# A planned transformer block on one core: 15 attention tiles moved from VectorE to ScalarE, weight copies moved off GpSimd, and a new instruction order

## The chip, the cores and the metric

The kernel runs on one core of a Trainium2 chip. The metric is the device time of one execution in microseconds (us), as a median of several executions. PE is TensorE (matrix products), ACT is ScalarE (exponentials, GELU, copies), DVE is VectorE, POOL is GpSimd, SP is the engine that issues the transfers.

## The reference, cut to what matters

One sequence of 2048 rows by 640 columns in bf16 goes through attention with 32 heads of 20 columns, then a gated feed-forward part of width 1728.

```python
x = A_x                                       # [1, 2048, 640]
qkv = layernorm(x) @ wqkv                     # 3 x 32 heads x 20
p = softmax(q @ k.T * 20 ** -0.5)             # per head, 2048 x 2048
h = x + (p @ v).reshape(1, 2048, 640) @ wo
g, u = layernorm(h) @ w_gate, layernorm(h) @ w_up      # 2048 x 1728
out = h + (gelu(g) * u) @ w_down
```

The scores are 32 x 2048 x 2048 numbers, and each goes through an exponential.

## The kernel before, in words

**Who sets the order.** The kernel is written as a list of operations with reads, writes, a duration and a priority (`op`). While the program is built, a planner (`Sched.schedule`) plays these through with its own durations, gives each engine a fixed order, hands out the 8 PSUM banks, and emits one stream for each engine with semaphore waits between them. On the chip each engine then runs its stream strictly in that order. So a planner number such as `c_dve` (VectorE), `c_act` (ScalarE) or the 0.222 us that it reckons for a group of score products adds no instruction; it only moves instructions within their streams. Priorities run from `P_QK` = 0 (first) over `P_PV` = 1 and `P_EPI` = 2 to `P_BG` = 3 (background).

**Tiling.** The query rows are cut into 7 chunks of 512, 512, 256, 256, 256, 128 and 128 rows (`CHUNKS`). The heads lie in 8 groups of 4, `g` = 0 to 7. A slot is one chunk of queries with as many head groups as fill 512 columns; there are 32 slots: 0 to 7 for chunk 0, 8 to 15 for chunk 1, then four each for the 256-row chunks and two each for the 128-row chunks. Each slot has 64 tiles of 128 keys x 512 columns, 2048 tiles in all. Consecutive tiles are joined to units of 2 or 3 tiles: a unit's score products (a "QK group" on PE) fill 2 or 3 banks, and one ACT instruction takes the exponential of the whole unit into bf16 (`pts`, or the second part of the ring in `rege`). Units alternate between banks 0 to 2 and banks 3 to 5. The string `PATS` says for each slot whether units alternate 3, 2 tiles ('2') or 3, 3 tiles ('3'). Where units are 3, 2, bank 5 is left to background work beside bank 7.

**VectorE tiles.** To relieve ACT, some tiles get their exponential on DVE from a polynomial on int16 bits (`d_exp`: one reading of PSUM for each tile, then seven instructions for a pair of tiles). The string `DS` gives their number for each slot (a hexadecimal digit), 217 of 2048 tiles in all; a unit of 3 with such a tile leaves a 2-tile exponential for ACT.

**Background.** While ACT takes exponentials, PE and DVE do everything else: `proj` makes the keys and queries of the next head group, `proj_v` the values, and `post` the output product, LayerNorm and feed-forward part of the chunk before. GELU of a chunk is done by ACT in one go, with a load of its function table before and after. Where PE has nothing to do, the planner fills in idle matmuls (`ps<-wo,gk`).

**Prologue.** Before the first QK group, all 16 blocks of 128 rows are normalised (statistics on the engines of `LNS`, scaling `LNE`), transposed on PE and copied out of PSUM (`LNV`: the copies `regw<-ps`) into `xnT`. Then `proj` makes the keys of head group 0 in four pieces (`k`, 0, 0 to 3) and the queries (`q`, 0, 0), on the engines of `G0E`; each key piece is squared (`sq`), summed by PE against `gk`, and its maximum (`kmx`, then `kq`, `fold`, `khalf`) is added to the queries, which the first QK group needs. The q and k weights come in packed at 20 columns a head and must lie at 32 columns a head (`wq_pad`, `wk_pad`). The function `pad` copies them: head group 0 early, the other 28 heads (`h0` = 4 to 32) in 5 pieces each for k and q, all on POOL, after the last scalings (`pad_ops`). These ten are called the weight copies below; `proj` of head group 1 needs all five of its kind.

```python
pad_ops.extend(x for x in e_ops[-8::2])
for dst, off, key in pads:
    for a in range(NA):
        pad(dst, off, 4, 32, key + "m", key, a, a + 1)
```

**Tail.** After the last exponential, the last chunk's 128 rows go through the output product, LayerNorm and feed-forward with nothing else to hide behind; ACT loads the tables for square root and GELU there.

Of the kernel before, what the change touches and what calls it, by code (L numbers as in the profile page):

```python
# [5 lines left out]
ACT = mybir.ActivationFunctionType  # L6
# [12 lines left out]
DMA_RATE = 0.36  # L19
DT = 0  # L20
LATE = (0, 1, 2, 3, 4)
LNS = [{'a': 'act', 'd': 'dve'}[x] for x in 'dddadddadddaddaa']
LNE = [{'a': 'act', 'd': 'dve'}[x] for x in 'adaadaaaadadaddd']
LNV = [{'a': 'act', 'd': 'dve'}[x] for x in 'ddddaddddddaddad']
SLIP = 0.0
WARM = 3.4
KEEP = 0.5
# [23 lines left out]
class Sched:  # L51
# [10 lines left out]
    def op(self, eng, fns, dur, prio, reads=(), writes=(), acq=(), rel=(), after=(), sem=None, lat=None, mode=None, mb=0.0, alt=None):  # L62
        if self.evp is not None and eng == "dve" and rel and prio >= P_EPI:
            prio = self.evp
        o = Op()
        o.i = len(self.ops)
        o.eng, o.dur, o.lat, o.sem = eng, dur, LAT[eng] if lat is None else lat, sem
        o.mode = mode
        o.mb = mb
        o.alt = alt  # L70
        o.tag = writes[0] if writes else None
        o.fns = fns if isinstance(fns, list) else [fns]
        o.prio = (prio, o.i)
        deps = set(after)
        for r in reads:
            if r in self.lw:
                deps.add(self.lw[r])
        for w in writes:
            if w in self.lw:
                deps.add(self.lw[w])  # L80
            deps.update(self.rd.get(w, ()))
        for r in reads:
            self.rd.setdefault(r, []).append(o.i)
        for w in writes:
            self.lw[w] = o.i
            self.rd[w] = []
        deps.discard(o.i)
        o.deps = deps
        o.acq = list(acq)
        o.rel = list(rel)  # L90
        o.succ = []
        o.ready = 0.0
        o.start = None
        o.group = None
        self.ops.append(o)
        return o.i
# [206 lines left out]
S = 2048  # L303
# [6 lines left out]
NA = D // 128  # L310
NG = H // 4
_cs = (512,512,256,256,256,128,128)
CHUNKS = tuple((sum(_cs[:i]), x) for i, x in enumerate(_cs))
# [15 lines left out]
P_QK, P_PV, P_EPI, P_BG = 0, 1, 2, 3  # L329
# [3 lines left out]
EVP = 2.5  # L333
PREC = 0
VH = 2
TFIRST = 0.0
PRE = 0.2
G0P = (2.5, 2.5, 2.5, 2.2, 2.2)
G0E = [{'a': 'act', 'd': 'dve'}[x] for x in 'aadaa']


def bass_sequential_preLN__mha_block__glu_gated_geglu__prompt_kernel(
# [12 lines left out]
    with ExitStack() as es:  # L355
        sc = Sched(nc)
        op = sc.op
# [4 lines left out]
        def I(method, *args, **kwargs):  # L362
            return lambda eng: getattr(eng, method)(*args, **kwargs)  # L363
# [6 lines left out]
            return 0.05 + n * 0.000833  # L370

        def c_dve(n, rate=1.04):
            return 0.064 + n * rate * 1e-3


        ident = sb("ident", [128, 128])
# [56 lines left out]
        wqk = carve(NA * 1280).rearrange("p (a d) -> p a d", a=NA)  # L433
# [35 lines left out]
        POOL = "pool"  # L469
# [52 lines left out]
        e_ops = []  # L522
        op("act", I("activation", nm[:, 0:1], off0[:], ACT.Sqrt), 0.06, -1, mode="sqrt", reads=["off0"], writes=["pre", ("nm", 0)])

        pad_ops = []

        def pad(dst, off, h0, h1, mkey, key, a0, a1):
            src = wqk[:, a0:a1, off + h0 * DH:off + h1 * DH].rearrange("p a (h e) -> p a h e", e=DH)
            e_ops.append(op(POOL, I("tensor_copy", dst[:, a0:a1, h0:h1, 1:21], src),
                            0.1 + (a1 - a0) * (h1 - h0) * DH * 0.0012, P_BG, reads=["wqk", mkey], writes=[key, "pool"],  # L530
                            after=pad_ops))

        pads = ((wk_pad, 640, "wkp"), (wq_pad, 0, "wqp"))
# [90 lines left out]
        for t0 in range(0, NT, 4):  # L624
# [3 lines left out]
            if sa:  # L628
                assert sa == list(range(sa[0], sa[-1] + 1))
                op("dve", I("tensor_scalar", mv[:, sa[0]:sa[-1] + 1, 1], mv[:, sa[0]:sa[-1] + 1, 1], 1.0 / D, None, ALU.mult), 0.14,  # L630
                   P_QK, reads=[("mv1", t) for t in sa], writes=[("mv", t) for t in sa])
# [5 lines left out]
                e_ops.append(len(sc.ops) - 2)  # L637


        pad_ops.extend(x for x in e_ops[-8::2])  # L640
        for dst, off, key in pads:
            for a in range(NA):
                pad(dst, off, 4, 32, key + "m", key, a, a + 1)

        w_readers = []

# [11 lines left out]
                    c_mm(n), prio, mode="col", alt=whole(lambda: bank(bk, n), l, r, k == 0, k == len(steps) - 1), reads=reads, writes=[key], acq=[bk] if (k == 0 and acq) else [],  # L658
                    after=after if k == 0 else ())

        def proj(which, g, c, banks, prio, evac="dve", early=False):
            wp, nm = (wk_pad, "k") if which == "k" else (wq_pad, "q")
            wkey = ("wkp" if which == "k" else "wqp") + ("0" if g == 0 else "")
            dst = kt_all[:, g, c * 512:(c + 1) * 512] if which == "k" else qt_all[:, c, g, :]
            bk = Bank(*banks)
            key = ("bk", sc_id())
# [4 lines left out]
            if evac == "act":  # L671
                if which == "k":
                    op("act", lambda eng: eng.activation(dst, bank(bk), ACT.Identity, bias=e0[:, 0:1]), c_act(512),
                       prio, reads=[key, "e0"], writes=[(nm, g, c)], rel=[bk])
                else:
                    op("act", lambda eng: eng.activation(dst, bank(bk), ACT.Copy), c_act(512), prio, reads=[key],
                       writes=[(nm, g, c)], rel=[bk])
            else:
                if which == "k":
                    op("dve", lambda eng: eng.tensor_scalar(dst, bank(bk), e0[:, 0:1], None, ALU.add), c_dve(512),  # L680
                       prio, reads=[key, "e0"], writes=[(nm, g, c)], rel=[bk])
# [5 lines left out]
               writes=[("sq", sqi)])  # L687
# [61 lines left out]
            tiles += [(s_, g, kb, j) for g in gs for kb in range(NT // nk) for j in range(4)]  # L749
            slot_end.append(len(tiles))  # L750

        PATS = '22222222222322232222222222322322'
        DS = '06518868658678897868898988658866'
        PAT = [((0, 1, 2), (3, 4, 5)) if PATS[i] == '3' else ((0, 1, 2), (3, 4)) for i in range(len(slots))]
        units, ubank, upos = [], [], []
        i = 0
# [55 lines left out]
        def unit(u):  # L812
# [16 lines left out]
            for kk in range(4):  # L829
                for i, (s_, g, kb, j) in enumerate(tl):  # L830
                    c = slots[s_][0]
                    q0, nq = CHUNKS[c]
                    if kk >= 512 // nq:
# [4 lines left out]
                                 qt_all[32 * j:32 * j + 32, q0 // 512, g, q0 % 512:q0 % 512 + nq],  # L838
                                 start=True, stop=True, tile_position=(32 * j, 0), skip_group_check=True))
                    reads += [("k", g, kt // 4), ("q", g, q0 // 512)]  # L840
            qk = op("pe", fns, 0.222, P_QK, mode="row", reads=reads, writes=[("S", u), "qkseq"] + ([("SD", tl[2])] if dt else []),
                            acq=bks)
            for x in tl:
                last_qk[slots[x[0]][0]] = qk
# [254 lines left out]
        for c in range(4):  # L1099
            proj("k", 0, c, PRO, G0P[c], G0E[c], True)  # L1100
        proj("q", 0, 0, PRO, G0P[4], G0E[4], True)
        for kt in range(NT):
            proj_v(kt, 0, (6, 7), P_BG, "dve", after=(sc.lw["q", 0, 0],) if kt >= VH else ())
        ui = 0
# [72 lines left out]
```

## Time and profile before

| | before |
|---|---|
| median of 3 runs | 944.24 us (943.75 to 944.79) |
| the profiled execution | 943.99 us, of which the span is 941.8 us |
| ACT busy | 902.9 us (96%) |
| PE busy | 882.1 us (94%) |
| DVE busy | 806.4 us (86%) |
| POOL busy | 18.0 us (2%) |

The span runs from the first to the last instruction of the program; 2.2 us of the profiled execution lie around it. Shares of busy time are averages over the prologue (to the first exponential at 34.5 us), the exponentials (to 914.5 us) and the tail. In a timeline each row merges instructions of one kind: start, length, count and, in brackets, how long the engine stood idle before it and for whom. Instructions of one engine overlap a little at their ends, so a mean length is longer than the distance from start to start.

### The profile page before, as it was taken

The numbers are of one execution on the slowest core, as the hardware profiler recorded it, in microseconds if no ns is written. First come the engines' busy times: TensorE is split into PE (matmuls) and PEld (weight loads), VectorE is DVE, ScalarE is ACT, GpSimd is POOL, SyncE is SP. The second block draws the span as 40 slices with busy tenths as digits, with TensorE's granted clock in tenths as the row PEclk, the third lists the DMA queues.
The fourth block names the chain that finished last, engine by engine and source line by source line (L and its number), as shares of the span: only waits on it lengthen the run. The fifth ranks groups of instructions, "written<-read, shape, count | busy, mean of one in ns | idle before, by whom it ended". The sixth has DMA issues, their size and how long they took to land.

```text
span 941.8 us, 33723 instructions
## 1 busy us (share of the span) xinstructions
PE 882.1 (94%) x15332; PEld 387.8 (41%) x15334; DVE 806.4 (86%) x1798; ACT 902.9 (96%) x885; POOL 18.0 (2%) x54
## 2 busy tenths in 40 slices
PE   4999999999999989999999999999999999989998
PEld 3433332222232222323343333344445455556766
DVE  7759868999999988798999887999999876998764
ACT  7699999999999999999999999999999999999981
POOL 4300000000000000000000000000000000000000
PEclk9999999999999999999999999999999999999999
DMA  7010000000000070000010000000000000000000
GB/s 251 2 30 2 2 1 2 2 1 2 1 2 2 9 276 1 1 2 16 12 34 1 2 2 2 2 9 24 9 23 3 9 3 24 18 17 5 4 15 18
DMA packets 11774, 19.92 MB, mean 21 GB/s; under 512 B 561, under 2 KB 9713, under 8 KB 11633
## 3 DMA queue, kind: packets, MB, share of 16 engines
q1 hardware_dynamic: 11632, 17.78, 5.7%
q8 instruction: 120, 1.97, 0.9%
q14 instruction: 22, 0.17, 0.1%
HBM read 15.16 MB, written 2.62 MB: 19 GB/s over the span
## 4 chain that ended last, share of the span: by engine, by line
ACT 75%; PE 14%; DVE 10%; DMA 1%; issue 0%; SPq 0%
ACT pts L363 44%; ACT rege L363 30%; PE ps L652 5%; PE ps L363 5%; DVE rege L363 3%; PE ps L648 3%; DVE qt_all L363 2%; DVE rege L1062 1%; DMA rege<-in_A_x_dram 1%; DVE rege L1074 1%; PE ps L602 1%; DVE stats L363 1%; ACT L363 1%; DVE rege L612 0%; DVE sq L363 0%
## 5 line engine op out<-in xcount | busy, mean ns | idle before, releaser
L363 ACT ACTIVATE pts<-ps 128x1024 bf16<-128x1024 f32 (+1 forms) x491 | 550.0, 1331 | 9.1 <-PE ps L363 8.9
L363 ACT ACTIVATE rege<-ps 128x1024 bf16<-128x1024 f32 (+1 forms) x312 | 361.7, 1325 | 0.4 <-PE ps L363 0.3
L363 PE MATMUL ps<-qt_all,kt_all 32*128 32x256 bf16 (+2 forms) x3584 | 314.9, 288 | 33.6 <-ACT pts L363 14.8
L363 PEld LDWEIGHTS ps<-qt_all,kt_all 32*128 32x128 bf16 x3584 | 98.1, 92 | 273.5 <-ACT pts L363 126.0
L652 PE MATMUL ps<-rege,regw 128*32 128x256 bf16 (+2 forms) x3046 | 161.1, 306 | 6.0 <-ACT rege L363 3.0
L363 PE MATMUL ps<-pts,v_all 128*21 128x256 bf16 (+2 forms) x1956 | 160.1, 292 | 0.1
L363 PE MATMUL ps<-rege,v_all 128*21 128x256 bf16 (+2 forms) x1396 | 128.7, 294 | 0.0
L652 PE MATMUL ps<-regw 128*32 128x512 bf16 (+1 forms) x1720 | 122.2, 356 | 0.6 <-DVE v_all L735 0.4
L363 DVE TENSOR_TENSOR rege<-rege 128x1024 bf16<-128x1024 bf16 (+2 forms) x173 | 113.6, 660 | 0.9
L363 DVE TENSOR_SCALAR rege<-rege 128x1024 bf16<-128x1024 int16 (+3 forms) x229 | 91.3, 408 | 1.6
L652 PEld LDWEIGHTS ps<-rege,regw 128*32 128x32 bf16 x3046 | 74.0, 96 | 39.4 <-issue 15.1
L363 DVE TENSOR_SCALAR qt_all<-ps 128x512 int16<-128x512 f32 x110 | 75.4, 686 | 10.8 <-PE ps L363 10.4
L363 DVE TENSOR_TENSOR qt_all<-qt_all 128x1024 bf16<-128x1024 bf16 (+3 forms) x121 | 80.8, 668 | 1.0
L363 DVE TENSOR_SCALAR rege<-ps 128x512 int16<-128x512 f32 x107 | 73.3, 685 | 9.6 <-PE ps L363 9.1
L652 PE MATMUL ps<-regw,rege 128*32 128x320 bf16 x1524 | 77.1, 301 | 0.7 <-DVE rege L1074 0.5
L363 DVE TENSOR_SCALAR qt_all<-qt_all 128x1024 int16<-128x1024 int16 (+3 forms) x178 | 71.7, 411 | 1.2
L363 PEld LDWEIGHTS ps<-pts,v_all 128*21 128x21 bf16 x1956 | 47.5, 90 | 61.0 <-issue 51.5
L363 PEld LDWEIGHTS ps<-rege,v_all 128*21 128x21 bf16 x1396 | 37.7, 90 | 42.0 <-issue 36.1
L363 PE MATMUL ps<-wo,gk 128*21 128x256 bf16 x297 | 52.7, 274 | 0.0
L652 PEld LDWEIGHTS ps<-regw 128*32 128x32 bf16 x1720 | 38.3, 95 | 34.0 <-issue 15.2
L1074 DVE TENSOR_TENSOR rege<-rege,ps 128x512 bf16<-128x512 bf16 (+2 forms) x53 | 36.0, 679 | 13.2 <-PE ps L652 12.8
L652 PEld LDWEIGHTS ps<-regw,rege 128*32 128x32 bf16 x1524 | 36.5, 95 | 23.8 <-issue 12.5
(109 smaller groups left out, 740.9 us busy)
## 6 DMA issues: line engine op xcount, KB each, us to landing
rege<-in_A_x_dram SPq DMA_DIRECT2D x5, 640.0 KB, 6.6
out_dram<-rege SPq DMA_DIRECT2D x16, 160.0 KB, 2.6
regw<-in_B_w_gate_dram SPq DMA_DIRECT2D x1, 2160.0 KB, 8.3
regw<-in_B_w_up_dram SPq DMA_DIRECT2D x1, 2160.0 KB, 13.3
regw<-in_B_w_down_dram SPq DMA_DIRECT2D x1, 2080.0 KB, 19.7
rege<-in_A_x_dram SPq DMA_DIRECT2D x5, 320.0 KB, 3.4
rege<-in_A_wqkv_dram SPq DMA_DIRECT2D x1, 1600.0 KB, 12.7
regw<-in_A_wqkv_dram SPq DMA_DIRECT2D x1, 800.0 KB, 14.3
```

The source lines that it names most:

```text
L363: return lambda eng: getattr(eng, method)(*args, **kwargs)
L602: op("pe", lambda eng, a=a: eng.transpose(bank16(bk, D)[:, 128 * a:128 * a + 128], src[:, a * 128:(a + 1) * 128], ident[:]), 0.056, prio, ...
L648: return [lambda eng: eng.matmul(out()[0:l.shape[-1]], l, r, start=start, stop=stop, skip_group_check=True)]
L652: return [lambda eng, j=j: eng.matmul(out()[j:j + 32], l[:, j:j + 32], r, start=start, stop=stop, tile_position=(0, j), skip_group_check=T ...
L1062: cp.append(op("dve", lambda eng, bg=bg, fv=fv, m=m, w_=w_: eng.tensor_copy(fv, bank(bg, w_)[0:m, :]), c_dve(w_), pre, reads=[kg], writes= ...
L1074: hdone.append(op("dve", lambda eng, bu=bu, fv=fv, m=m, w_=w_: eng.tensor_tensor(fv, fv, bank(bu, w_)[0:m, :], ALU.mult), c_dve(w_), p, re ...
```

## The change

It does five things. The number of VectorE tiles falls from 217 to 202 and four more slots (5, 16, 17, 21) get units of 3, 3 tiles. In the prologue, the split of LayerNorm statistics, scalings and copies between ACT and DVE is chosen anew, and so are the engines and priorities of head group 0's projections. The ten late weight copies leave POOL: eight go to ACT (after the last key piece of head group 0), two to DVE (after the queries of head group 0). The planner reckons QK groups of 256-row chunks at 0.25 us and of 128-row chunks at 0.295 us, where it had 0.222 us for all, and a fixed part of 0.07 us for DVE where it had 0.064 us. `proj` gives its ACT and DVE operations the priority `KPR`, whose value 3.0 is that of `P_BG`.

```diff
-LNS = [{'a': 'act', 'd': 'dve'}[x] for x in 'dddadddadddaddaa']
-LNE = [{'a': 'act', 'd': 'dve'}[x] for x in 'adaadaaaadadaddd']
-LNV = [{'a': 'act', 'd': 'dve'}[x] for x in 'ddddaddddddaddad']
+LNS = [{'a': 'act', 'd': 'dve'}[x] for x in 'dddaddaaddddddaa']
+LNE = [{'a': 'act', 'd': 'dve'}[x] for x in 'daaadaaaadadaddd']
+LNV = [{'a': 'act', 'd': 'dve'}[x] for x in 'ddadadddddaaddaa']
...
+PADE = 'aaaaaaaadd'
+KPR = 3.0
...
-G0P = (2.5, 2.5, 2.5, 2.2, 2.2)
-G0E = [{'a': 'act', 'd': 'dve'}[x] for x in 'aadaa']
+G0P = (2.5, 2.5, 2.5, 2.2, 1.5)
+G0E = [{'a': 'act', 'd': 'dve'}[x] for x in 'addaa']
...
         def c_dve(n, rate=1.04):
-            return 0.064 + n * rate * 1e-3
+            return 0.07 + n * rate * 1e-3
...
-        def pad(dst, off, h0, h1, mkey, key, a0, a1):
+        def pad(dst, off, h0, h1, mkey, key, a0, a1, eng=POOL):
             src = wqk[:, a0:a1, off + h0 * DH:off + h1 * DH].rearrange("p a (h e) -> p a h e", e=DH)
+            if eng != POOL:
+                fn = I("activation", dst[:, a0:a1, h0:h1, 1:21], src, ACT.Copy) if eng == "act" else I("tensor_copy", dst[:, a0:a1, h0:h1, 1:21], src)
+                e_ops.append(op(eng, fn, 0.65 if eng == "act" else 0.35, P_BG, reads=["wqk", mkey], writes=[key], after=pad_ops))
+                return
...
-        pad_ops.extend(x for x in e_ops[-8::2])
-        for dst, off, key in pads:
-            for a in range(NA):
-                pad(dst, off, 4, 32, key + "m", key, a, a + 1)
...
-        def proj(which, g, c, banks, prio, evac="dve", early=False):
+        def proj(which, g, c, banks, prio_, evac="dve", early=False):
+            op = lambda eng, fn, dur, p, **kw: sc.op(eng, fn, dur, prio_ if eng == "pe" or early else KPR, **kw)
+            prio = prio_
...
-        PATS = '22222222222322232222222222322322'
-        DS = '06518868658678897868898988658866'
+        PATS = '22222322222322233322232222322322'
+        DS = '06318768667678897767888886647565'
...
-            qk = op("pe", fns, 0.222, P_QK, mode="row", reads=reads, writes=[("S", u), "qkseq"] + ([("SD", tl[2])] if dt else []),
+            qk = op("pe", fns, {512: 0.222, 256: 0.25, 128: 0.295}[CHUNKS[slots[tl[0][0]][0]][1]], P_QK, mode="row", reads=reads, writes=[("S", u), "qkseq"] + ([("SD", tl[2])] if dt else []),
...
         proj("q", 0, 0, PRO, G0P[4], G0E[4], True)
+        k3 = sc.lw["k", 0, 3]
+        for dst, off, key in pads:
+            for a in range(NA):
+                e_ = PADE[a + NA * (key == "wqp")]
+                pad_ops[:] = [sc.lw["q", 0, 0] if e_ == "d" else k3]
+                pad(dst, off, 4, 32, key + "m", key, a, a + 1, "dve" if e_ == "d" else "act")
```

## The prediction

> **What bounds the kernel now.** I read the page's line of busy times first, then the busy times by stage, cut where the exponentials begin and end and behind the first slot and before the last ones (stretch, its length, then busy time and count of PE, PE's weight loads, DVE, ACT and POOL); after that the timelines of each place where ACT stands idle.
>
> ```profile
> PE 882.1 (94%) x15332; PEld 387.8 (41%) x15334; DVE 806.4 (86%) x1798; ACT 902.9 (96%) x885; POOL 18.0 (2%) x54
> ```
>
> ```profile
> 0.00:34.50 34.50, 19.99 (x162) 12.31 (x164) 29.06 (x98) 22.99 (x43) 18.00 (x54) 1.00 0.51 172
> 34.50:66.80 32.30, 31.62 (x568) 13.15 (x567) 16.25 (x37) 28.67 (x25) 0.00 (x0) 1.00 0.01 3
> 66.80:850.00 783.20, 745.28 (x12249) 301.80 (x12248) 701.64 (x1537) 782.79 (x750) 0.00 (x0) 1.00 0.05 17
> 850.00:914.50 64.50, 61.09 (x2052) 41.71 (x2047) 47.49 (x102) 62.64 (x59) 0.00 (x0) 1.00 0.02 7
> 914.50:941.80 27.30, 24.13 (x311) 18.86 (x308) 12.01 (x27) 5.83 (x10) 0.00 (x0) 1.00 0.06 19
> ```
>
> From 66.8 to 850 us ACT is busy for 782.79 of 783.20 us. ScalarE is the bound there, without slack: work added to it lengthens the run one for one, and work taken from PE, DVE or POOL there is worth nothing. ACT's idle time among the exponentials is 3.63 us (34.5 to 66.8), 0.41 us and 1.86 us, together 5.9 us. That, the 34.5 us before and the 27.3 us after are all that a better order can win.
>
> **Part 1: 15 tiles from DVE to ACT (the largest term).** ACT's instructions from 34.5 to 914.5 us, grouped by shape (count | busy us, mean ns | idle before), price one exponential:
>
> ```profile
> L363 ACT ACTIVATE pts<-ps 128x1024 bf16<-128x1024 f32 x349 | 371.1, 1210 | 3.4 <-PE ps L363 3.2
> L363 ACT ACTIVATE rege<-ps 128x1024 bf16<-128x1024 f32 x227 | 246.0, 1210 | 0.4 <-PE ps L363 0.3
> L363 ACT ACTIVATE pts<-ps 128x1536 bf16<-128x1536 f32 x141 | 228.2, 1634 | 5.7 <-PE ps L363 5.7
> L363 ACT ACTIVATE rege<-ps 128x1536 bf16<-128x1536 f32 x85 | 137.0, 1633 | 0.0
> L363 ACT ACTIVATE rege<-rege 128x2048 bf16<-128x2048 bf16 x9 | 16.8, 1903 | 0.1
> L363 ACT ACT_TABLE_LOAD x13 | 16.7, 1283 | 0.2
> L363 ACT ACTIVATE rege<-rege 128x1536 bf16<-128x1536 bf16 x3 | 4.4, 1467 | 0.0
> L363 ACT ACTIVATE rege<-rege 128x1792 bf16<-128x1792 bf16 x1 | 1.7, 1697 | 0.0
> L363 ACT ACTIVATE rege<-rege 64x512 bf16<-64x512 bf16 x2 | 1.2, 614 | 0.0
> L363 ACT ACTIVATE rege<-rege 128x512 bf16<-128x512 bf16 x2 | 1.2, 614 | 0.0
> L363 ACT ACTIVATE pts<-ps 128x512 bf16<-128x512 f32 x1 | 0.6, 597 | 0.0
> ```
>
> Three tiles take 0.424 us longer than two (1634 - 1210 ns). ACT is busy for 28.67 + 782.79 + 62.64 = 874.1 us in these stages; GELU, table loads and the single-tile one take 16.8 + 16.7 + 4.4 + 1.7 + 1.2 + 1.2 + 0.6 = 42.6. The rest, 831.5 us, is 576 exponentials of 2 tiles and 226 of 3: 802 a + 226 x 0.424 gives a = 0.917 us from start to start for 2 tiles, and 1.341 us for 3. The mean lengths are about 0.3 us more because neighbours overlap; I add that overlap to each idle time below, since a wait seen as idle also loses it.
>
> In the instruction order of the two built programs, exponentials of 2 tiles fall from 576 to 509 and those of 3 rise from 226 to 276; one of a single tile goes. That is -67 x 0.917 + 50 x 1.341 - 0.5 = +5.1 us on ACT. Table loads (16) and GELU instructions are the same in both. DVE loses 15 tiles, but no ACT time waits for it here, so that is worth nothing by itself. The four slots with units of 3, 3 tiles take bank 5 from background work; PE has ACT's longer instruction to hide behind, and I cost that at nothing (if the one bank 7 is too narrow, it shows as idle ACT in slots 5, 16, 17 or 21).
>
> **Part 2: the prologue and the weight copies.** The end of the prologue on ACT with one row of PE, and below it what DVE and POOL do meanwhile:
>
> ```profile
> 23.58 0.20 ACT L363 ACTIVATE sd<-sd 128x4 bf16<-128x4 bf16 x1
> 23.69 0.69 ACT L609 ACTIVATE regw<-ps 128x640 bf16<-128x640 bf16 x1
> 24.28 0.68 ACT L673 ACTIVATE kt_all<-ps,e 128x512 bf16<-128x512 f32 x1
> 24.85 0.92 ACT L363 ACTIVATE rege<-rege,nm,rs 128x640 bf16<-128x640 bf16 x1
> 28.68 0.69 ACT L673 ACTIVATE kt_all<-ps,e 128x512 bf16<-128x512 f32 x1 [1.74 <-PE ps L648]
> 29.38 1.28 ACT L363 ACT_TABLE_LOAD   x1
> 34.52 2.37 ACT L363 ACTIVATE pts<-ps 128x1536 bf16<-128x1536 f32 x2 [3.86 <-PE ps L363]
> 38.36 1.45 ACT L363 ACTIVATE pts<-ps 128x1536 bf16<-128x1536 f32 x1 [1.47 <-PE ps L363]
> 39.70 2.36 ACT L363 ACTIVATE rege<-ps 128x1024 bf16<-128x1024 f32 x2
> ...
> 34.61 3.38 PE L652 MATMUL ps<-regw 128*32 128x512 bf16 x84
> ```
>
> ```profile
> 29.28 1.65 DVE L363 TENSOR_TENSOR sq<-kt_all 128x512 bf16<-128x512 bf16 x2
> 31.48 0.41 DVE L363 TENSOR_TENSOR sq<-qt_all 128x512 bf16<-128x512 bf16 x1
> 33.39 0.64 DVE L363 TENSOR_SCALAR qt_all<-qt_all,khalf 128x512 bf16<-128x512 bf16 x1
> 25.89 7.99 POOL L363 COPY regw<-rege 128x560 bf16<-128x560 bf16 x10 [8.60 <-ACT rege L363]
> ```
>
> While POOL copies (25.89 to 33.88), two squarings of the same shape take 0.82 us each instead of 0.41, and one small addition takes 0.64 us; all lie on the way to the first QK group. With POOL silent, I take 0.4 us off the last squaring and about 0.3 off the addition.
>
> Against that, ACT has more to do before its last key piece: the order shows six `regw<-ps` copies there instead of three (0.59 us each, 23.69 to 24.28) and one `kt_all` less (0.57). After the last square root (`sd`) stand in a row a copy, a `kt_all`, another copy, a scaling (0.92) and two more copies. From 23.7, with some 0.6 us of wait for the first transposes, that is 24.3 + 0.6 + 0.6 + 0.6 + 0.9 + 1.2 = 28.2 us. The five products of the last key piece follow: four quarter products take 0.16 us in the PE row (3.38 us for 84), whole ones of 512 columns rather more, so I take 1.3 us with the start. Then `kt_all` starts at about 29.5 (28.68 before) and ends at 30.2. Here the order puts six weight copies before the table load. No such copy on ACT is in the trace. Its nearest rows are the copy of 640 columns (0.59) and the `kt_all` of 512 (0.57); for 560 columns I take 0.52 and keep 0.45 to 0.6. So 30.2 + 6 x 0.52 + 1.29 = 34.6 us for the first exponential, against 34.52: the idle 3.86 us is filled, not won. The first QK group itself comes earlier (about 33.1: 0.8 late, then 0.4 + 0.4 + 0.3 and a shorter queue on DVE back) and is hidden.
>
> The third exponential waits for PE in both: between QK group 2 and 3 lie 84 products of the background before and 92 after (3.38 and about 3.7 us). That gives about 37.7 instead of 38.36. Then the order has the last two weight copies on ACT (2 x 0.52), since the next exponential writes `rege`, where the packed weights lie; it starts at 37.7 + 1.33 + 1.04 = 40.1, against 39.70. **Start and copies together: +0.4 us** (-0.7 to +1.4). The two DVE copies stand behind three value copies, long before anyone needs the query weights.
>
> [...]
>
> **Part 3: the turn from slot 0 to slot 1.**
>
> ```profile
> 62.11 2.56 ACT L363 ACTIVATE rege<-ps 128x1024 bf16<-128x1024 f32 x2
> 66.80 2.37 ACT L363 ACTIVATE pts<-ps 128x1024 bf16<-128x1024 f32 x2 [2.14 <-PE ps L363]
> ...
> 63.63 1.35 PE L652 MATMUL ps<-regw 128*32 128x320 bf16 x32
> 64.81 0.40 PE L652 MATMUL ps<-sq,gqh 128*32 128x512 bf16 x4
> 66.37 0.60 PE L363 MATMUL ps<-qt_all,kt_all 32*128 32x512 bf16 x5
> ```
>
> ACT stands idle for 2.14 us because slot 1's first QK group needs the queries of head group 1, and their last product (`sq,gqh`) was queued behind 32 background products. In the new order `sq,gqh` stands three QK groups ahead of the turn, and 288 instead of 320 value products come before it. PE then can have the group at about 63.4 us (66.4, less 1 us for the earlier start, 1.35 us for the 32 products and 0.7 us of PE's own waits, 32.30 - 31.62). ACT is done with slot 0 at 62.11 + 0.92 + 1.34 = 64.4, 0.4 later in the new run, and wants the group 0.4 us before that. **-2.4 us** (2.14 + 0.3 of overlap), with about 0.9 us to spare before it is PE again that is late.
>
> **Part 4: the last slots.**
>
> ```profile
> 896.32 1.94 ACT L363 ACTIVATE pts<-ps 128x1024 bf16<-128x1024 f32 x2 [0.87 <-PE ps L363]
> 904.89 4.46 ACT L363 ACTIVATE pts<-ps 128x1536 bf16<-128x1536 f32 x4 [0.38 <-PE ps L363]
> 914.49 1.28 ACT L363 ACT_TABLE_LOAD   x1
> 915.78 0.20 ACT L363 ACTIVATE nm<-off 128x1 f32<-128x1 f32 x1
> ```
>
> ACT idles for 1.86 us here (64.50 - 62.64), nearly all in these two waits and a smaller one; with the overlap lost at the larger two that is 2.4 us. The longer QK durations make the planner leave PE earlier for them; but the new order also has a longer background block at the last GELU (174 products against 109). I take half: **-1.2 us** (-2.4 to +1.2). In the tail PE has 36 products of 320 columns instead of 34 and 45 of 128 instead of 51 between the last exponential and the final feed-forward, and two transposes stand earlier in its queue: **-0.3 us** (-0.8 to +0.5).
>
> The planner's DVE constant adds no instruction, and `KPR` equals the priority it replaces: nothing.
>
> **The sum.** +5.1 + 0.4 - 2.4 - 1.2 - 0.3 = +1.6 us on a span of 941.8 and an execution of 943.99 us. That execution is 0.25 us under the median, so the median goes from 944.24 to 945.8 us. A measurement of this kernel can hardly tell less than 0.2% (1.9 us) from no change; the forecast is no change, on the slow side.
>
> **The rivals.** *PE's waits move instead of going* (slower). PE is 94% busy, and in slot 0 it never rests (31.62 of 32.30 us). If its blocks run longer than I reckoned by more than the 0.9 us to spare at the turn, ACT waits there again: with all of the 2.4 us back the time is 948.2, with the last slots unchanged too 949.4. For it speaks that one bank less in four slots and a longer GELU block press on PE; against it the order of `sq,gqh`. *The first table load costs more between work than in idle time*: its 1.28 us twice over would be +1.3, so 947.1; the loads among the exponentials speak against it. [...] *All idle goes*: the start 0.7 early, 2.4 and 2.4 won, the tail -0.8, so 5.1 - 0.7 - 2.4 - 2.4 - 0.8 = -1.2, 943.0. *The small waits go too* (faster): the fixed part of an exponential is 0.917 - 2 x 0.424 = 0.069 us; if a tenth of it is waiting that ends where QK groups come earlier, 785 x 0.007 = 5.5 us go, and the sum gives 940.3. Nothing in the views says that these hundredths are waits.
>
> **How the numbers follow.** The forecast, from 944.4 to 947, 0.45; waits that move, 947 to 949.5, 0.28; the dearer load 0.05; all idle gone 0.10; small waits gone 0.12. Slower by over 0.2% (above 946.1): 0.28 + 0.05 + 0.09 of the forecast's upper end = 0.42. Within: 0.36 + 0.10 = 0.46. Faster: 0.12. The range runs from 942.6 to 949.0; it leaves out most of the last case and the top of the second. The likeliest case alone has 944.4 to 947.
>
> **What would show it.** Part 1 is right if the shapes count 509 and 276 and their start-to-start stays at 0.917 and 1.341. Part 2: six copies of 128x560 on ACT at about 0.52 us after 30 us, first exponential near 34.6, fourth near 40.1. Part 3: no idle ACT over 0.3 us between 60 and 70 us. Part 4: ACT idle after 850 us at about half of 1.86. I am wrong if ACT shows more than 3 us idle after its fourth exponential, or if 3-tile exponentials come closer together than 1.33 us.

## The result and the profile after

The changed kernel takes 948.16 us (median of 5 runs, 947.80 to 948.22) against 944.24 us; ratio 1.0041 with a 95% interval of 1.0026 to 1.0056. It is slower by 3.9 us. The likeliest forecast (945.8, no change that can be measured) was wrong; the time lies in the range, on the number of the first rival (948.2).

The profiled execution took 948.16 us with a span of 946.3 us, 4.5 us longer than the span before. First the line of busy times, then the busy times by stage, cut as before where the exponentials begin and end:

```profile
PE 878.0 (93%) x15284; PEld 383.5 (41%) x15286; DVE 781.8 (83%) x1740; ACT 913.8 (97%) x877; POOL 10.6 (1%) x44
```

```profile
0.00:34.50 34.50, 20.35 (x185) 12.62 (x191) 28.10 (x97) 27.13 (x51) 10.62 (x44) 1.00 0.51 172
34.50:66.80 32.30, 31.38 (x561) 12.95 (x553) 15.89 (x36) 31.94 (x30) 0.00 (x0) 1.00 0.04 8
66.80:850.00 783.20, 737.87 (x12127) 295.79 (x12123) 678.08 (x1478) 780.96 (x728) 0.00 (x0) 1.00 0.05 16
850.00:919.10 69.10, 64.44 (x2137) 43.69 (x2130) 48.41 (x105) 67.94 (x63) 0.00 (x0) 1.00 0.04 11
919.10:946.30 27.20, 23.93 (x298) 18.49 (x295) 11.37 (x26) 5.81 (x10) 0.00 (x0) 1.00 0.06 19
```

ACT took on 10.9 us, DVE gave up 24.6 us. ACT's idle time fell from 3.63 to 0.36 us up to 66.8 us and from 1.86 to 1.16 us at the end, but rose from 0.41 to 2.24 us in the long middle, where those 0.41 us had been all there was to win. The end of the exponentials moved by 4.6 us (the table load behind the last one from 914.49 to 919.07, last fence of this section); the tail stayed at 27.2 us (27.3 before). So the whole loss lies ahead of the last exponential.

The groups of ACT in the exponential stage:

```profile
L365 ACT ACTIVATE pts<-ps 128x1024 bf16<-128x1024 f32 x314 | 341.2, 1235 | 1.9 <-PE ps L365 1.8
L365 ACT ACTIVATE pts<-ps 128x1536 bf16<-128x1536 f32 x170 | 273.2, 1659 | 1.2 <-PE ps L365 1.1
L365 ACT ACTIVATE rege<-ps 128x1024 bf16<-128x1024 f32 x195 | 218.2, 1232 | 0.3 <-PE ps L365 0.3
L365 ACT ACTIVATE rege<-ps 128x1536 bf16<-128x1536 f32 x106 | 172.2, 1664 | 0.0
```

509 exponentials of 2 tiles and 276 of 3, as the order said. Busy time in the three stages is 31.94 + 780.96 + 67.94 = 880.8 us; GELU, table loads and the two late copies are 43.4 of it. The rest gives 785 a + 276 x 0.424 = 837.4, so a = 0.918 us (0.917 before). The mean lengths rose by 25 ns (1235 against 1210) and the distances did not: mean length is no price.

The start on ACT, and DVE's part of the way to the first QK group:

```profile
29.27 0.69 ACT L677 ACTIVATE kt_all<-ps,e 128x512 bf16<-128x512 f32 x1 [1.75 <-PE ps L650]
29.99 3.47 ACT L365 ACTIVATE regw<-rege 128x560 bf16<-128x560 bf16 x6
33.48 1.28 ACT L365 ACT_TABLE_LOAD   x1
34.77 2.36 ACT L365 ACTIVATE pts<-ps 128x1536 bf16<-128x1536 f32 x2
37.35 1.45 ACT L365 ACTIVATE pts<-ps 128x1536 bf16<-128x1536 f32 x1 [0.21 <-PE ps L365]
38.69 1.37 ACT L365 ACTIVATE regw<-rege 128x560 bf16<-128x560 bf16 x2
40.10 2.36 ACT L365 ACTIVATE rege<-ps 128x1024 bf16<-128x1024 f32 x2
```

```profile
29.99 0.42 DVE L365 TENSOR_TENSOR sq<-kt_all 128x512 bf16<-128x512 bf16 x1 [0.40 <-ACT kt_all L677]
32.72 0.35 DVE L365 TENSOR_SCALAR qt_all<-qt_all,khalf 128x512 bf16<-128x512 bf16 x1
```

The turns. ACT goes from slot 0 to slot 1 without idle time (64.91), but stands idle at the next turn, from slot 1 to slot 2 (92.89). Below it PE's stream at that second turn:

```profile
62.68 2.56 ACT L365 ACTIVATE rege<-ps 128x1024 bf16<-128x1024 f32 x2
64.91 4.42 ACT L365 ACTIVATE pts<-ps 128x1024 bf16<-128x1024 f32 x4
...
90.45 1.61 ACT L365 ACTIVATE pts<-ps 128x1536 bf16<-128x1536 f32 x1
92.89 2.37 ACT L365 ACTIVATE pts<-ps 128x1024 bf16<-128x1024 f32 x2 [0.83 <-PE ps L365]
```

```profile
90.18 0.40 PE L654 MATMUL ps<-sq,gqh 128*32 128x512 bf16 x4
90.77 0.40 PE L365 MATMUL ps<-rege,v_all 128*21 128x512 bf16 x4 [0.19 <-ACT rege L365]
91.20 0.86 PE L654 MATMUL ps<-regw 128*32 128x320 bf16 x20
92.46 0.60 PE L365 MATMUL ps<-qt_all,kt_all 32*128 32x512 bf16 x5 [0.40 <-DVE qt_all L723]
```

The product `sq,gqh` for head group 2 now stands ahead of the first QK group that needs it with no QK group between (values and background products alone), and that group waits for DVE to add its result to the queries. With the overlap of 0.29 us lost, the turn costs 1.1 us. In the kernel before, four QK groups lay between, and ACT passed this turn (93.4 us) in the middle of a row without idle time:

```profile
88.10 0.39 PE L652 MATMUL ps<-sq,gqh 128*32 128x512 bf16 x4
...
92.05 3.93 ACT L363 ACTIVATE pts<-ps 128x1536 bf16<-128x1536 f32 x3
```

One more new wait, at 339 us, and the end:

```profile
335.49 2.67 ACT L365 ACTIVATE pts<-ps 128x1536 bf16<-128x1536 f32 x2
339.06 1.45 ACT L365 ACTIVATE pts<-ps 128x1536 bf16<-128x1536 f32 x1 [0.90 <-PE ps L365]
...
890.99 2.37 ACT L365 ACTIVATE pts<-ps 128x1024 bf16<-128x1024 f32 x2 [0.60 <-PE ps L365]
900.63 1.28 ACT L365 ACT_TABLE_LOAD   x1
901.93 1.70 ACT L365 ACTIVATE rege<-rege 128x1792 bf16<-128x1792 bf16 x1
919.07 1.28 ACT L365 ACT_TABLE_LOAD   x1
```

### The profile page after: what moved, and what is told of

It reads as the page before. It is cut to its first block, busy times and chain, and to the rows that moved or that the text cites. A ratio compares the mean times of both kernels' runs of the same rounds, so it can differ in the third digit from the quotient of the medians.

```text
span 946.3 us, 33533 instructions
## 1 busy us (share of the span) xinstructions
PE 878.0 (93%) x15284; PEld 383.5 (41%) x15286; DVE 781.8 (83%) x1740; ACT 913.8 (97%) x877; POOL 10.6 (1%) x44
## 4 chain that ended last, share of the span: by engine, by line
ACT 84%; PE 11%; DVE 3%; DMA 1%; issue 0%; SPq 0%
ACT pts L365 50%; ACT rege L365 33%; PE ps L654 4%; PE ps L650 3%; PE ps L365 3%; DVE rege L365 1%; ACT L365 1%; DMA rege<-in_A_x_dram 1%; PE ps L608 1%; PE ps L942 0%; DVE kt_all L684 0%; DVE v_all L739 0%; ACT xn_t L365 0%; DVE sq L365 0%; DVE qt_all L723 0%
## 5 line engine op out<-in xcount | busy, mean ns | idle before, releaser
L365 ACT ACTIVATE pts<-ps 128x1024 bf16<-128x1024 f32 (+1 forms) x484 | 560.3, 1384 | 3.1 <-PE ps L365 3.0
L365 PE MATMUL ps<-qt_all,kt_all 32*128 32x256 bf16 (+2 forms) x3584 | 307.9, 289 | 41.7 <-ACT pts L365 15.8
L654 PE MATMUL ps<-rege,regw 128*32 128x256 bf16 (+2 forms) x3070 | 164.7, 306 | 6.3 <-ACT rege L365 2.3
L365 DVE TENSOR_TENSOR rege<-rege 128x1024 bf16<-128x1024 bf16 (+3 forms) x165 | 106.0, 645 | 1.5
L654 PEld LDWEIGHTS ps<-rege,regw 128*32 128x32 bf16 x3070 | 74.2, 96 | 40.1 <-issue 15.7
L365 DVE TENSOR_SCALAR rege<-rege 128x1024 bf16<-128x1024 int16 (+3 forms) x218 | 85.3, 399 | 1.9
L365 DVE TENSOR_SCALAR qt_all<-ps 128x512 int16<-128x512 f32 x105 | 72.0, 686 | 14.3 <-PE ps L365 13.7
L365 DVE TENSOR_SCALAR rege<-ps 128x512 int16<-128x512 f32 x97 | 66.5, 685 | 12.8 <-PE ps L365 12.6
L365 DVE TENSOR_TENSOR qt_all<-qt_all 128x1024 bf16<-128x1024 bf16 (+2 forms) x113 | 75.7, 670 | 1.5
L365 DVE TENSOR_SCALAR qt_all<-qt_all 128x1024 bf16<-128x1024 int16 (+3 forms) x167 | 67.8, 413 | 1.4
L365 PEld LDWEIGHTS ps<-rege,v_all 128*21 128x21 bf16 x1378 | 37.9, 90 | 41.2 <-issue 34.5
L365 PE MATMUL ps<-wo,gk 128*21 128x256 bf16 x249 | 44.1, 276 | 0.6 <-DVE qt_all L723 0.6
```

Of the source, the lines that this page charges most:

```text
L654: return [lambda eng, j=j: eng.matmul(out()[j:j + 32], l[:, j:j + 32], r, start=start, stop=stop, tile_position=(0, j), skip_group_check=T ...
```

## The experiments

The texts on record use these names. *Theory 1* (later *A*): the parts add up as the prediction reckoned them, so undoing one gives its term back. *Theory 2*: PE's waits move whenever the order is planned anew, so a part undone does not give its term back. *Theory 3* (later *C*), formed after the first four runs: the place of the last GELU among the exponentials decides. *Theory B*, formed after eight: the waits at the turns follow from how far ahead of its turn each product for the queries stands. Runs of one group shared their runs of the kernel before: 945.05 us (11 runs) for the first four, 945.18 (9) for the next four, 944.43 (27) for the last four.

### Undoing one part of the change, or doing one alone

**The old tiles in the changed kernel.**

```diff
-        PATS = '22222322222322233322232222322322'
-        DS = '06318768667678897767888886647565'
+        PATS = '22222222222322232222222222322322'
+        DS = '06518868658678897868898988658866'
```

> The changed kernel with the 217 VectorE tiles and the unit pattern of before; all else of the change stays. Theory 1 (the change costs what it adds to ACT): the exponentials get shorter by 5.1 us, so 943.1 us, between 942 and 944.5. Theory 2 (the new order brought waits, the tiles cost little net): most of the loss stays, 946.5 to 948.5.

Measured: 963.16 us, ratio to before 1.0185 (1.0171 to 1.0200). Neither theory has a place for this. The end of its ACT timeline:

```profile
911.42 2.88 ACT L365 ACTIVATE pts<-ps 128x1536 bf16<-128x1536 f32 x3
914.31 1.28 ACT L365 ACT_TABLE_LOAD   x1
...
928.47 1.70 ACT L365 ACTIVATE rege<-rege 128x1792 bf16<-128x1792 bf16 x1 [2.23 <-DVE rege L1066]
```

The exponentials end at 914.3, 4.8 us earlier than in the changed kernel. (5.1 us of exponentials are gone from their stage, and a GELU of 1.7 with two table loads of 1.3; the rest went into new waits, the largest 4.2 us at 831.) But the GELU of the last chunk but one (128x1792), which the kernels before and after have at 899.6 and 901.9 among the exponentials, now comes 14 us behind the last of them. That chunk's feed-forward part then stands in the tail: 45.7 us from the table load to the end of the span of 960.0.

**The new tiles in the kernel before.**

```diff
-        PATS = '22222222222322232222222222322322'
-        DS = '06518868658678897868898988658866'
+        PATS = '22222322222322233322232222322322'
+        DS = '06318768667678897767888886647565'
```

> The kernel before with nothing but the 202 VectorE tiles and the unit pattern of after. Theory 1: 944.2 + 5.1 = 949.3 us, between 948 and 951, with 509 and 276 exponentials and ACT still waiting 2 us at the turn from slot 0 to slot 1. Theory 2: 944 to 946.

Measured: 955.37 us, ratio 1.0100 (1.0085 to 1.0115). Tail 27.0 us. The fourth exponential comes at 41.2 us (39.7 before); the mean granted clock of this execution was 0.996, against 1.00 in the one before, and how much of the delay comes from that was not shown. The turn still costs 2.5 us, and there are new waits, 1.35 us of idle time at 911, 1.26 at 747 and 0.97 at 920 the largest. The tiles alone cost 10.3 us against 945.05, 5 more than their 5.1; the one execution with a mean clock of 1.00 took 953.26.

**The old QK length in the changed kernel.**

```diff
-            qk = op("pe", fns, {512: 0.222, 256: 0.25, 128: 0.295}[CHUNKS[slots[tl[0][0]][0]][1]], P_QK, ...
+            qk = op("pe", fns, 0.222, P_QK, ...
```

> The changed kernel with the planner's old 0.222 us for every QK group; no instruction differs in kind. Theory 1: within 1.5 us of 948.2, as the planner's numbers move only waits of a few tenths. Theory 2: the waits near 90 and 337 us are the new lengths' doing and go, so 946 or less.

Measured: 949.84 us, ratio 1.0048 (1.0034 to 1.0062). That is 1.7 us from the changed kernel, a little outside theory 1's 1.5 and far from theory 2's 946 or less; the wait near 90 us, which theory 2 had going, is still there (1.1 us). Exponentials end 2.4 us later than in the changed kernel and the tail is 1.7 us shorter. So the reckoning of the small chunks is worth little by itself here. PE's order is the same up to the small chunks, and this execution has no wait at 339 us.

**The weight copies back on POOL in the changed kernel.**

```diff
+        pad_ops.extend(x for x in e_ops[-8::2])
+        for dst, off, key in pads:
+            for a in range(NA):
+                pad(dst, off, 4, 32, key + "m", key, a, a + 1)
...
-        k3 = sc.lw["k", 0, 3]
-        for dst, off, key in pads:
...
```

> The changed kernel with the ten late weight copies back on GpSimd, at their old place in the program. Theory 1: ACT loses 8 copies of about 0.57 us, but six of them filled idle time; the first QK group comes about 1 us later through slower VectorE operations and the fourth exponential starts at 39.5 to 40.3 us as now: 947.2 to 948.5. Rival (the two copies between exponentials cost their full 1.4 us): 946.6 or less, fourth exponential before 39.0 us.

Measured: 963.34 us, ratio 1.0188 (1.0174 to 1.0203). The fourth exponential is at 39.87, where theory 1 had it; the time is not. ACT at the first turn:

```profile
62.20 2.63 ACT L365 ACTIVATE rege<-ps 128x1024 bf16<-128x1024 f32 x2
68.99 2.37 ACT L365 ACTIVATE pts<-ps 128x1024 bf16<-128x1024 f32 x2 [4.17 <-PE ps L365]
```

The turn costs 4.6 us, another wait of 3.3 us stands at 742 us, and the last GELU comes at 926.0, behind the last exponential (918.5): a tail of 42.2 us.

### Moving the last GELU

**One tile more in slot 10 of the changed kernel** (its order puts the last GELU behind all 785 exponentials).

```diff
-        DS = '06318768667678897767888886647565'
+        DS = '06318768668678897767888886647565'
```

> The changed kernel with one VectorE tile more (slot 10: 8 instead of 7; 203 tiles). In its instruction order the GELU of the last but one chunk slides behind the last exponential, as in the two kernels that took 963 us. Theory 3 (the time is the end of the exponentials plus a tail, and the tail is about 27 us where that GELU comes among the exponentials and over 40 us where it does not): last exponential near 919, tail over 40, 961 to 964 us. Theory 1 alone (ACT's added work decides): one tile less on ACT, 947.8 us, between 947 and 949.

Measured: 958.53 us, ratio 1.0139 (1.0125 to 1.0154), with exponentials until 915.5 and a tail of 42.1 us. One tile fewer for ACT, and the run is 10 us longer: theory 3 is right in kind and its range 2.5 us too high, because the exponentials end 3.6 us earlier with one GELU and its tables gone from their stage.

**Five tiles more, placed so that the last GELU keeps seven exponentials behind it.**

```diff
-        DS = '06318768667678897767888886647565'
+        DS = '06318868667678897767898888648565'
```

> The changed kernel with five VectorE tiles more (slots 5, 21 and 28 one each, slot 25 two; 207 tiles); in its order the last GELU still stands seven exponentials ahead of the end. Theories 1 and 3: 5 x 0.424 off the exponentials, less at most 1 us of new waits, so 946.4 us, between 945.5 and 947.5. A theory by which more VectorE tiles themselves delay the background: 950 or more.

Measured: 952.54 us, ratio 1.0075 (1.0063 to 1.0088): missed by 6 us. The exponentials end at 919.6, no earlier than in the changed kernel: what five tiles win is eaten by new waits of 1.0 us (200), 0.6 (444), 1.9 (639) and 1.3 us (914). The tail has 31.8 us. The time fits the last theory of the text, by which more VectorE tiles themselves delay the background; no run here tells that from the waits that any new order brings.

**Two more copies on DVE in the changed kernel.**

```diff
-PADE = 'aaaaaaaadd'
+PADE = 'aaaaaadddd'
```

> The changed kernel with the last two ACT weight copies on VectorE too (four there, six on ACT). Theory 1: the 1.41 us between the third and the fourth exponential go, so the fourth starts at 38.7 us and the time is 946.8, between 946.3 and 947.5. Rival (PE is late with the next QK group or VectorE with the copies): the fourth exponential starts at 39.5 or later and the time stays at 948.

Measured: 949.32 us, ratio 1.0039 (1.0024 to 1.0053). The fourth exponential comes 0.5 us earlier instead of 1.4, as the rival of the text had it, and the turn from slot 0 to slot 1 takes more than that back:

```profile
39.61 2.37 ACT L365 ACTIVATE rege<-ps 128x1024 bf16<-128x1024 f32 x2
...
67.95 2.37 ACT L365 ACTIVATE pts<-ps 128x1024 bf16<-128x1024 f32 x2 [3.33 <-PE ps L365]
```

**The new QK lengths alone, in the kernel before.**

```diff
-            qk = op("pe", fns, 0.222, P_QK, ...
+            qk = op("pe", fns, {512: 0.222, 256: 0.25, 128: 0.295}[CHUNKS[slots[tl[0][0]][0]][1]], P_QK, ...
```

> The kernel before with nothing but the planner's longer QK groups (0.25 and 0.295 us). Its order has the last GELU behind the last exponential. Theory 3: exponentials end near 914 as before, tail over 40: 956 to 960 us. Theory 1 alone: no work is added to ACT, 944 to 945.

Measured: 956.16 us, ratio 1.0113 (1.0097 to 1.0128). ACT does the same work as before, with two table loads fewer; only the order differs.

```profile
905.29 2.88 ACT L363 ACTIVATE pts<-ps 128x1536 bf16<-128x1536 f32 x3
...
922.06 1.70 ACT L363 ACTIVATE rege<-rege 128x1792 bf16<-128x1792 bf16 x1 [1.63 <-DVE rege L1062]
```

Exponentials end at 908.2, 6 us earlier than before, and the run is 11 us longer, since the last GELU comes 14 us behind them. Theory 3 gave the kind from the order alone; that its range holds the time is partly luck, since it had the exponentials end near 914 and the tail, which is 46.1 us, just over 40. Over all kernels, the exponentials that the order leaves behind the last GELU against the tail (from the end of the last exponential):

| | behind the last GELU | tail, us |
|---|---|---|
| old QK length in the changed kernel | 18 | 25.5 |
| new tiles in the kernel before | 15 | 27.0 |
| after; two more copies on DVE | 13 | 27.2; 27.2 |
| before, and the last four kernels below | 11 | 27.3; 27.3 |
| five tiles more | 7 | 31.8 |
| old tiles; copies on POOL; one tile more; QK lengths alone | 0 | 45.7; 42.2; 42.1; 46.1 |

### The turns

In the built orders one can count how many whole QK groups stand between a product for the queries (`sq,gqh`) and the first QK group that needs it, which opens the new slot. The table has this number for the first three turns and, behind a colon, what the turn costs in the trace (idle time and the overlap lost, us; no entry: no wait):

| | turn to slot 1 | to slot 2 | to slot 3 |
|---|---|---|---|
| before | 0: 2.5 | 4 | 1 |
| after | 1 | 0: 1.1 | 3 |
| old tiles | 1 | 0: 1.1 | 0: 2.5 |
| new tiles in the kernel before | 0: 2.5 | 4 | 4 |
| old QK length | 1 | 0: 1.1 | 3 |
| copies on POOL | 0: 4.6 | 4 | 5 |
| two more copies on DVE | 0: 3.7 | 6 | 7 |
| QK lengths alone | 0: 2.4 | 4 | 1 |
| copies alone | 1 | 0: 1.0 | 0: 2.5 |
| all copies on ACT | 2 | 0: 1.1 | 1 |
| prologue split alone | 0: 4.5 | 4 | 1 |
| prologue split and copies | 0: 1.0 | 0: 1.1 | 1 |

In all 36 cases a turn waits when the product stands directly ahead of the group that needs it, and only then; one group between them is enough. The two kernels that the table leaves out (one tile more, five tiles more) have the order and the waits of the changed kernel at these turns. The turns to slots 4 to 7 of all fourteen kernels keep to the rule too: one of them has no group between, the turn to slot 6 with five tiles more, and it alone waits (the 1.0 us at 200 us). The first eight rows gave the rule, and the last four kernels were run to try it: variants of the kernel before in which the last GELU keeps its place. Their texts on record count merged rows of the stream ("behind 23, 50 and 74 QK groups") and set the bound at three groups; the count above is the sharper one, and calls for a wait at the same turns.

**The copies alone**: the kernel before with the weight copies of the changed kernel.

```diff
+PADE = 'aaaaaaaadd'
...
-        pad_ops.extend(x for x in e_ops[-8::2])
-        for dst, off, key in pads:
...
+        k3 = sc.lw["k", 0, 3]
+        for dst, off, key in pads:
...
```

> The kernel before with one part of the change: the ten late weight copies leave POOL, eight to ACT and two to DVE, as in the changed kernel. DVE tiles, prologue split and planner numbers are those of before. In the instruction order the last GELU keeps 11 exponentials behind it, and the product for the queries (sq,gqh) of head groups 1, 2 and 3 stands behind 23, 50 and 74 QK groups. Theory A (the part stands for itself): the wait of 2.14 us at the turn from slot 0 to slot 1 goes and nothing comes in its place; 945.0 - 2.2 = 942.8 us. Theory B (the order is planned anew as a whole, and what counts is whether each product stands at least three QK groups ahead of its turn): no wait near 63 us, 1.1 us near 90 us (as in every run so far with 50), 2.5 us near 118 us (as in the one run so far with 74); 945.0 + 0.1 - 2.4 + 1.1 + 2.5 = 946.3 us (945.5 to 947.5). Theory C (the last GELU slides, tail over 40 us) says tail 27 us here, so nothing above 949.

Measured: 944.20 us, ratio 0.9998 (0.9989 to 1.0007).

```profile
64.46 4.42 ACT L364 ACTIVATE pts<-ps 128x1024 bf16<-128x1024 f32 x4
...
92.22 2.37 ACT L364 ACTIVATE pts<-ps 128x1024 bf16<-128x1024 f32 x2 [0.61 <-PE ps L364]
...
120.41 1.45 ACT L364 ACTIVATE pts<-ps 128x1536 bf16<-128x1536 f32 x1 [2.18 <-PE ps L364]
```

No wait at the first turn, 1.0 us at the second and 2.5 at the third: the three places and sizes are theory B's, and theory A's 942.8 is out. The time is 2 us below B's sum, though: 0.6 of it is the base (945.0, where the kernel before took 944.43 in this group), the waits behind 850 us are 1.0 us shorter than before, and the start did not cost the 0.1 (fourth exponential at 39.59).

**All ten copies on ACT**, shown against the kernel just told of.

```diff
-PADE = 'aaaaaaaadd'
+PADE = 'aaaaaaaaaa'
```

> The kernel before with all ten late weight copies on ACT, none on DVE or POOL; all else as before. The products for the queries stand behind 22, 50 and 73 QK groups; seven copies are ahead of the first exponential, three ahead of the fourth. Theory A: two more ACT copies than the previous kernel, about 1.4 us more: 944.2 us. Theory B: no wait near 63 us, 1.1 us near 90 us, none near 118 us: 945.0 + 1.0 - 2.4 + 1.1 = 944.7 us (943.8 to 945.8), so less than the previous kernel although ACT has two copies more. Tail 27 us by both.

Measured: 943.77 us, ratio 0.9990 (0.9982 to 0.9999), and faster than the changed kernel. That it is faster than before by a tenth of a per cent is not shown to be the copies' doing: all its runs had a mean PE clock of 1.00, and the 17 runs of the kernel before that had it too (last section) have a median of 944.1 us, 0.3 away.

```profile
38.62 1.93 ACT L364 ACTIVATE regw<-rege 128x560 bf16<-128x560 bf16 x3
40.58 2.37 ACT L364 ACTIVATE rege<-ps 128x1024 bf16<-128x1024 f32 x2
...
65.59 4.42 ACT L364 ACTIVATE pts<-ps 128x1024 bf16<-128x1024 f32 x4
...
93.45 2.37 ACT L364 ACTIVATE pts<-ps 128x1024 bf16<-128x1024 f32 x2 [0.71 <-PE ps L364]
```

0.9 us more at the start, nothing at the first turn, 1.1 us at the second, nothing at the third: +0.9 - 2.5 + 1.1 = -0.5 us, the difference of the spans (941.3 and 941.8, both at a mean clock of 1.00). The time alone can't tell theory A's 944.2 from theory B's 944.7; the places of the waits do, and they are B's. Two copies more on ACT, and the time does not grow.

**The prologue split alone**, the copies still on POOL.

```diff
-LNS = [{'a': 'act', 'd': 'dve'}[x] for x in 'dddadddadddaddaa']
-LNE = [{'a': 'act', 'd': 'dve'}[x] for x in 'adaadaaaadadaddd']
-LNV = [{'a': 'act', 'd': 'dve'}[x] for x in 'ddddaddddddaddad']
+LNS = [{'a': 'act', 'd': 'dve'}[x] for x in 'dddaddaaddddddaa']
+LNE = [{'a': 'act', 'd': 'dve'}[x] for x in 'daaadaaaadadaddd']
+LNV = [{'a': 'act', 'd': 'dve'}[x] for x in 'ddadadddddaaddaa']
...
-G0P = (2.5, 2.5, 2.5, 2.2, 2.2)
-G0E = [{'a': 'act', 'd': 'dve'}[x] for x in 'aadaa']
+G0P = (2.5, 2.5, 2.5, 2.2, 1.5)
+G0E = [{'a': 'act', 'd': 'dve'}[x] for x in 'addaa']
```

> The kernel before with the new prologue split alone (LNS, LNE, LNV, G0P, G0E of the changed kernel); the late weight copies stay on POOL. Products for the queries behind 24, 45 and 73 QK groups, as before. Theory A: POOL still slows DVE's squarings, so the first QK group and the fourth exponential (39.9 to 40.4 us) are as late as before or by 0.5 later; 945.0 to 945.6 us. Theory B: the wait near 63 us stays, between 2.1 and 4.6 us (what runs with 24 showed), none near 90 us; 945.0 to 948 us. Tail 27 us by both.

Measured: 947.83 us, ratio 1.0047 (1.0033 to 1.0060), at the upper end of theory B's range.

```profile
70.47 2.37 ACT L363 ACTIVATE pts<-ps 128x1024 bf16<-128x1024 f32 x2 [4.17 <-PE ps L363]
```

The turn costs 4.5 us, 2.1 more than before. The fourth exponential comes at 41.3, 0.9 us later than either theory allowed; the last section shows why in this execution. The one execution with a mean clock of 1.00 took 947.83 as well.

**Prologue split and copies**, that is the change without its tiles, QK lengths and DVE constant; against the kernel just told of:

```diff
+PADE = 'aaaaaaaadd'
...
-        pad_ops.extend(x for x in e_ops[-8::2])
...
+        k3 = sc.lw["k", 0, 3]
...
```

> The kernel before with the new prologue split and the late weight copies as in the changed kernel, that is the change without its tiles, QK durations and DVE constant. Products for the queries behind 24, 49 and 72 QK groups. Theory A: start and turn as in the changed kernel, 945.0 + 0.3 - 2.4 = 942.9 us. Theory B: the wait near 63 us comes back with 2.1 to 4.6 us since the product stands two QK groups ahead and not three, and up to 0.8 us near 90 us; 945 to 948.5 us. Tail 27 us by both.

Measured: 945.53 us, ratio 1.0020 (1.0011 to 1.0029).

```profile
41.55 2.37 ACT L364 ACTIVATE rege<-ps 128x1024 bf16<-128x1024 f32 x2
...
67.18 3.28 ACT L364 ACTIVATE pts<-ps 128x1024 bf16<-128x1024 f32 x3 [0.61 <-PE ps L364]
```

Waits at the first turn (1.0 us) and the second (1.1), where theory B had them, the first smaller than in any earlier run. So the order tells whether a turn waits; it does not tell for how long. With the start 1.85 us later, which neither theory had and no run explains, 1.5 us less at the first turn, 1.1 more at the second and 0.4 less later it makes +1.1, which is the difference measured.

## Why the prediction was wrong in its likeliest case, and right in its range

**Part 1 held** (+5.1 us): counts and distances as stated. It is the bulk of the loss, and only on ACT's path: DVE's 24.6 us bought nothing that ends late.

**Part 2 held** (+0.4): the fourth exponential comes at 40.10 (forecast 40.1, before 39.70), the first at 34.77 (34.6). The copies were mis-sized, 0.58 us from start to start ahead of the load and 0.70 behind the exponentials instead of 0.52; the third exponential, at 37.35 instead of 37.7, made up for it. With POOL silent the last squaring of the keys took 0.42 us and the addition 0.35, as taken. In the kernel before, though, three other squarings (27.2, 27.5 and 31.5 us) took 0.42 us while POOL copied, and the POOL copies that started during two of them (27.33 and 31.51 us) took 1.10 and 0.91 us instead of 0.66. The two squarings that took 0.86 and 0.87 us (29.28 and 30.06) began 0.07 and 0.13 us after a POOL copy had started (29.21 and 29.93). The table load was followed 1.29 us after its start (33.48 to 34.77), now between busy instructions, so the second rival is out.

**Part 3 is the step that failed.** It was right on the turn it looked at: no idle time between 60 and 70 us, -2.4. But it took that turn for the only one. In the order of the changed kernel the product for slot 2 stands right at its turn, where the kernel before had four QK groups between; that is +1.1, and it could be read in the order before any run, by the same count that part 3 made for slot 1. Of the three groups that part 3 counted ahead of the first turn, one stands between the product and the group that needs it; it was enough. Of the 3.0 us by which the sum fell short of the profiled span (1.6 against 4.6 below), this step is 1.1; the two paragraphs that follow have 0.6 and 1.3.

**Part 4 and the tail** were a little too hopeful: ACT idles 1.16 us behind 850 us instead of 1.86, 0.8 us with the overlap instead of 1.2, and the tail from the table load is 0.1 us shorter, not 0.3.

**A wait without a place in the sum**: 0.90 us of idle time at 339 us, 1.3 with the overlap lost in the two rows there. The last section shows that PE ran at half rate there (granted clock 0.50); the one timed execution of the changed kernel whose mean clock was 1.00 took 947.80, so how much of the median this is stays open, from 0.4 us to all of it.

Together: 1.6 + 1.1 + 1.3 + 0.4 + 0.2 = 4.6 us, where the span grew by 4.5. The median grew by 3.9, as 0.3 us less lie around the span and the profiled execution before lay 0.25 us under its median. By the prediction's own sign (more than 3 us of idle ACT after the fourth exponential: 2.24 + 1.16 = 3.4) its main case is wrong, if narrowly: 0.90 us of that idle time is the wait at PE's half rate. The first rival was right in kind, but not in its place: it had the wait come back at the same turn because PE's blocks ran long, and the wait came back one turn later because a product was planned later. That its number, 948.2, is the time measured is luck: it has 2.4 us for the turn, where 1.1 came at a turn, 1.3 at half rate and 0.6 at the end. The third rival falls with the idle time that stayed, the last with the distance of 0.918 us, which did not move.

**What the change's parts are worth.** With the last GELU in place, copies alone are worth nothing measurable, prologue and copies together +1.1 us, and tiles, QK lengths and DVE constant take the kernel from there to 948.2. Tiles and QK lengths cannot be had one at a time: the new lengths with the old tiles push the last GELU behind the exponentials (956 to 963 us), and the new tiles bring it back at the price of part 1. Why the GELU slides is argued, not shown: projections, weight loads and feed-forward parts of the chunks follow one another in the background, and a planner that reckons PE busier places the last of them too late. What sets the length of a wait at a turn (1.0 to 4.6 us with no group between) stays open as well.

## What to carry to other kernels

Where a planner orders the instructions, a changed constant is a new order: before reckoning what a part is worth, read in the built order every place of the kind that the old trace shows waiting (here each turn, and the last GELU), not only the place that the change is to mend. Price work on the bound engine by the distance from start to start, not by mean length. Parts of such a change do not add up, so take one apart only among variants in which the end of the run has the same shape.

## What the runs showed of the hardware

In the profiled execution of the changed kernel the clock granted to PE was 0.50 for 3.41 us, from 335.48 to 338.89 us. PE in the changed kernel, and in the one with the old QK length, whose order is the same there; then, in the changed kernel, the stretch of the fall and the one ahead of it (behind the five engines, the granted clock):

```profile
337.21 1.27 PE L654 MATMUL ps<-rege,regw 128*32 128x512 bf16 x8
```

```profile
336.74 0.63 PE L654 MATMUL ps<-rege,regw 128*32 128x512 bf16 x8
```

```profile
332.06:335.48 3.42, 2.57 (x25) 0.96 (x21) 2.21 (x4) 3.42 (x4) 0.00 (x0) 1.00 1.03 408
335.48:338.89 3.41, 3.41 (x23) 0.90 (x21) 2.40 (x6) 2.68 (x3) 0.00 (x0) 0.50 1.05 369
```

The same eight products take 1.27 us at a granted clock of 0.50 and 0.63 us with the old QK length, where the clock was 1.00 from 330 to 345 us. The prologue split alone had a mean granted clock of 0.89 from 30 to 45 us, and there 84 background products between the second and the third QK group took 4.95 us instead of the 3.38 before, which made its fourth exponential late.

```profile
34.66 4.95 PE L652 MATMUL ps<-regw 128*32 128x512 bf16 x84
```

In the stretch ahead of the fall PE was busy for 2.57 of 3.42 us at a clock of 1.00. What brings a fall on was not shown.

A lower granted clock can pass for an effect of the kernel: of the 27 runs of the kernel before, 17 with a mean clock of 1.00 took 943.4 to 944.8 us, 8 with 0.998 took 944.6 to 946.3, and 2 with 0.996 took 946.7 and 947.0. The two kernels that move the copies and nothing else had 1.00 in all 22 runs.
